# A new instruction order for a fused attention and feed-forward kernel, with one weight load issued later

## The chip, the cores and the metric

The kernel runs on one core of a Trainium2 chip. The metric is the device time of one execution in microseconds (us), as a median of several runs. Profiles are single executions; their span is 1.2 to 1.9 us shorter than the device time of the same run. The engines are TensorE (PE in the profile; PEld is its weight load), VectorE (DVE), ScalarE (ACT), GpSimd (POOL) and SyncE (SP). A "q" behind an engine's name (SPq, ACTq) is its issuing of transfers.

## The reference, cut to what matters

```python
x  = A_x                                    # 2048 x 448, bf16
xn = layernorm(x)
q, k, v = split(xn @ wqkv)                  # 16 heads of 28
pq, pk  = q @ w_phi, k @ w_phi              # per head
phi     = concat(softmax(p), softmax(-p))   # for pq and pk
o       = (phi_q @ (phi_k.T @ v)) / (phi_q @ sum(phi_k))
out     = x + o @ wo + silu(xn @ w1) @ w2   # w1: 448 x 1792
```

x is cut into 16 tiles of 128 rows. "The head" below is the start of the program, until the first three 256-column blocks of `xn @ w1` are done for tiles 0 to 3. It ends with three pairs of 64-row matmuls. "The fold" multiplies w_phi into the transposed q and k weights, about 27 us into the program.

## The kernel before

The program builds a list of operations and orders them itself. Each engine has an in-order list; PE's list follows a written plan from the end of the head. The plan's words: `aF3@4` and `bF3` are the two halves of block 3 of `xn @ w1` in PSUM banks 4 and 5; `aq`, `ak`, `av` are projections; `f2@0` is a part of the fold; `s` and `U` are parts of the attention; `W` and `R` belong to the output projection.

The first loads, in order of issue:

```python
load_x(0, 1); load_x(1, 2); load_x(2, 4)
load(w1_sb[:, 0:2, 0:512], ...,  "w1_0")    # first piece, first half,  256 KB, SP
load(w1_sb[:, 2:4, 0:512], ...,  "w1_0r")   # first piece, second half, 256 KB, SP
load_w1(512, 1024, "act")                   # second piece: "w1_512", 384 KB, ACT;
                                            # its last rows, 128 KB, SP
load_x(4, 8)                                # "x4": 448 KB, SP
load_w1(1024, FF)                           # 768 KB, SP
load_rows4(wv_sb, A_wqkv, 2*D, 3*D, "wv"); load_x(8, 12); ...
# [cut] four small loads of w_phi, issued by POOL at 3 to 6 us, behind "vaug1"
```

A `chain` fixes the order of the named operations on one engine. `ve0` to `ve3` are the standard deviations of tiles 0 to 3 (called variances below), `ev0` to `ev3` evict the transposed tiles:

```python
chain("warm_act w1_512 ve0 ve1 ev0a ev0 ev1 ve2 ve3 ev2 silu_table".split())
byname["w1_512"].deps.add(byname["warm_act"].id)
# [cut]
for word in "tr0a tr0 tr1 00a 10a 01a 11a 00b 10b 01b 11b tr2 20 21 tr3 02 12 22 03 13 23".split():
```

In this last line `tr1` transposes tile 1; `00a` is block 0, tile 0, with the first half of the first w1 piece, `00b` the same with its second half; `20` is block 2, tile 0, the first word that needs the second piece. The kernel before applies the first half to tiles 0 and 1, then the second half to both. ACT issues the second piece as soon as its warm-up is done.

## Time and profile before

| | before |
|---|---|
| median | 150.09 us (3 runs, 149.77 to 150.26) |
| span of the profiled run | 148.3 us |
| first matmul of block 20 | 8.45 us |
| end of the head (first 64-row matmul) | 11.45 us |
| from there to the start of the last matmul | 134.46 us |

Three more views are useful as a base. The first is the PE timeline of the head in the kernel before (start, busy us, engine, line, operation, output<-inputs, number of instructions):

```profile
8.23 0.39 PE L497 MATMUL psum<-ident,RA 128*128 128x128 bf16 x4
8.45 0.83 PE L482 MATMUL psum<-xnT,phT 128*128 128x128 bf16 x12
9.12 0.39 PE L497 MATMUL psum<-ident,RA 128*128 128x128 bf16 x4
9.34 4.03 PE L482 MATMUL psum<-xnT,phT 128*128 128x128 bf16 x50
```

Nothing waits: block 20 runs at 8.45, right behind the transposes of tile 2. The w1 pieces land in a buffer that the profile calls phT, because it is used again later. The second is the page's list of transfers, with KB each and us from issue to landing; this is the second w1 piece:

```profile
phT<-in_B_w_dram ACTq DMA_DIRECT2D x1, 384.0 KB, 4.6
```

The third is the table of stretches of the kernel before. After the stretch come its length, the busy time of PE, PEld, DVE, ACT and POOL, each with its instruction count, the granted TensorE clock, the DMA share and the GB/s:

```profile
4.00:6.00 2.00, 2.00 (x21) 1.77 (x18) 1.89 (x8) 0.88 (x4) 1.95 (x6) 1.00 1.00 335
6.00:8.00 2.00, 1.80 (x23) 1.41 (x22) 1.83 (x8) 1.28 (x4) 0.19 (x1) 1.00 1.08 342
8.00:11.00 3.00, 3.00 (x57) 3.00 (x55) 1.67 (x5) 2.08 (x3) 0.75 (x2) 1.00 1.05 361
11.00:16.00 5.00, 4.93 (x52) 2.29 (x51) 4.41 (x16) 3.77 (x4) 3.18 (x9) 1.00 1.35 256
```

PE is busy in full from 8 us on, and its clock is 1.00 in every stretch. (For the first stretches this column misleads: the trace has no clock event there, and until 6.6 us the matmuls of the head still start about 107 ns apart, later 56 ns.)

### The profile page before, as it was taken

What the parts mean: (1) busy time and instruction counts of PE and PEld (TensorE: products, weight loads), DVE (VectorE), ACT (ScalarE), POOL (GpSimd) and SP (SyncE); (2) the same over time, 40 slices, a digit from 0 to 9 for tenths busy, and PEclk for the clock granted to TensorE, in tenths of its full rate; (3) what the DMA queues carried; (4) which work ended last, traced back from release to release, by engine and by line L of the source; (5) the groups of instructions that cost most, each with busy time, mean ns of one, the idle gap of its engine ahead of it and who ended that gap; (6) DMA issues with size and microseconds to landing.
All of it is one profiled execution on the core that took longest, in us unless ns stands there. A gap on an engine that the chain in (4) does not pass through costs nothing.

```text
span 148.3 us, 3741 instructions
## 1 busy us (share of the span) xinstructions
PE 143.9 (97%) x1572; PEld 80.2 (54%) x1572; DVE 91.3 (62%) x197; ACT 71.8 (48%) x92; POOL 74.1 (50%) x92
## 2 busy tenths in 40 slices
PE   7999999999999999999999999999899999999994
PEld 7894444554544557646444445555455555545573
DVE  2968997380799399407992006995789544225083
ACT  4657656569994699995755599100040000000000
POOL 8628566501099999996999600996001800000000
DMA  4999954899930000000387490086899884305024
GB/s 104 337 359 239 301 106 78 165 117 250 348 96 0 0 0 4 4 0 4 63 153 142 81 136 0 0 164 88 155 210 183 111 156 95 70 4 186 0 68 154
DMA packets 44496, 17.53 MB, mean 118 GB/s; under 512 B 37040, under 2 KB 44096, under 8 KB 44480
## 3 DMA queue, kind: packets, MB, share of 16 engines
q1 hardware_dynamic: 41648, 15.10, 50.0%
q10 hardware_dynamic: 2704, 2.17, 4.8%
q8 instruction: 12, 0.20, 0.5%
q0 software_dynamic: 128, 0.03, 0.1%
q14 instruction: 4, 0.03, 0.1%
HBM read 6.57 MB, written 1.84 MB: 57 GB/s over the span
## 4 chain that ended last, share of the span: by engine, by line
PE 68%; DVE 11%; DMA 8%; SPq 6%; ACT 3%; issue 2%; POOL 1%; ACTq 0%
PE psum L482 68%; SPq L583 5%; DVE Rec L778 4%; DMA phT<-in_B_w_dram 3%; DMA vaug<-vaug 3%; DVE st L643 2%; DMA wT<-in_A_wqkv_dram 2%; DVE RA L658 1%; SPq L516 1%; ACT hT L502 1%; DVE Rec L779 1%; ACT L502 1%; ACT Ek_sb L502 1%; DVE mv L644 1%; DVE x_sb L896 1%
## 5 line engine op out<-in xcount | busy, mean ns | idle before, releaser
L482 PE MATMUL psum<-xnT,phT 64*128 64x512 bf16 (+1 forms) x428 | 45.5, 351 | 0.3 <-DMA phT<-in_B_w_dram 0.2
L482 PE MATMUL psum<-w_sb,hT 128*128 128x448 bf16 (+1 forms) x238 | 45.1, 342 | 0.0
L778 DVE TENSOR_REDUCE Rec<-Ek_sb 128x32 f32<-128x896 bf16 (+1 forms) x20 | 24.4, 1251 | 24.6 <-ACT Ek_sb L502 17.9
L814 POOL TENSOR_TENSOR RA<-Ek_sb,Rec 128x896 bf16<-128x896 bf16 x16 | 27.0, 1722 | 22.0 <-issue 12.0
L502 ACT ACTIVATE hT<-psum 128x1024 bf16<-128x1024 f32 x28 | 27.3, 1023 | 10.9 <-PE psum L482 10.9
L482 PEld LDWEIGHTS psum<-xnT,phT 64*128 64x128 bf16 (+1 forms) x428 | 21.5, 95 | 20.2 <-PE psum L482 0.6
L482 PEld LDWEIGHTS psum<-w_sb,hT 128*128 128x128 bf16 x238 | 22.2, 98 | 18.7 <-issue 1.5
L502 ACT ACTIVATE Ek_sb<-psum 128x864 bf16<-128x864 f32 x24 | 20.2, 915 | 19.1 <-PE psum L482 18.8
L482 PE MATMUL psum<-Wqk,xnT 64*128 64x432 bf16 x224 | 23.3, 343 | 0.1
L482 PEld LDWEIGHTS psum<-Wqk,xnT 64*128 64x128 bf16 x224 | 10.5, 95 | 10.1 <-issue 0.8
L788 POOL TENSOR_TENSOR Ek_sb<-Ek_sb,Rec 128x896 bf16<-128x896 bf16 x8 | 13.3, 1699 | 5.0 <-DVE Rec L779 5.0
L788 POOL TENSOR_TENSOR phT<-phT,Rec 128x896 bf16<-128x896 bf16 x8 | 13.4, 1702 | 0.2 <-DVE Rec L779 0.2
L482 PE MATMUL psum<-wv,xnT 64*128 64x448 bf16 x112 | 12.6, 349 | 0.1
L643 DVE BATCH_NORM_STATS2 st<-x_sb 128x6 f32<-128x448 bf16 x16 | 9.6, 603 | 2.9 <-DMA x_sb<-in_A_x_dram 2.9
L896 DVE TENSOR_TENSOR x_sb<-psum,x_sb 128x448 bf16<-128x448 f32 (+1 forms) x13 | 7.1, 582 | 6.6 <-PE psum L482 6.6
L482 PE MATMUL psum<-wo_sb,vaug 128*128 128x448 bf16 (+1 forms) x51 | 10.5, 341 | 0.5 <-DMA vaug<-vaug 0.5
L874 DVE TENSOR_SCALAR den<-psum 128x16 f32<-128x16 f32 x16 | 2.4, 157 | 13.2 <-PE psum L482 13.2
L881 DVE TENSOR_TENSOR vaug<-psum,rden 128x448 bf16<-128x448 f32 x16 | 9.8, 623 | 0.4
L658 DVE TENSOR_SCALAR RA<-x_sb,mv,rstd 128x384 bf16<-128x384 bf16 (+4 forms) x29 | 8.9, 346 | 1.3 <-POOL rstd L654 1.1
L779 DVE RECIPROCAL Rec<-Rec 128x32 f32<-128x32 f32 (+1 forms) x24 | 8.7, 393 | 0.2
L482 PEld LDWEIGHTS psum<-wv,xnT 64*128 64x128 bf16 x112 | 5.4, 94 | 5.5 <-PE psum L482 0.5
L502 ACT ACTIVATE vaug<-psum 128x896 bf16<-128x896 f32 x8 | 7.4, 923 | 1.7 <-PE psum L482 1.7
(59 smaller groups left out, 113.0 us busy)
## 6 DMA issues: line engine op xcount, KB each, us to landing
out_dram<-x_sb ACTq DMA_DIRECT2D x15, 112.0 KB, 1.7
w_sb<-in_B_w_dram SPq DMA_DIRECT2D x1, 1568.0 KB, 9.4
x_sb<-in_A_x_dram SPq DMA_DIRECT2D x3, 448.0 KB, 5.9
wo_sb<-in_A_wo_dram SPq DMA_DIRECT2D x2, 336.0 KB, 7.6
phT<-in_B_w_dram SPq DMA_DIRECT2D x1, 576.0 KB, 7.0
phT<-in_B_w_dram SPq DMA_DIRECT2D x2, 256.0 KB, 4.4
phT<-in_B_w_dram ACTq DMA_DIRECT2D x1, 384.0 KB, 4.6
wv<-in_A_wqkv_dram SPq DMA_DIRECT2D x1, 336.0 KB, 7.2
```

The lines of the kernel that those rows point to most:

```text
L482: r = e.matmul(dst, lhsT, rhs, start=st, stop=sp, skip_group_check=True)
L502: P.op("act", d_act(n), lambda e: e.activation(dst, src, func, scale=scale), reads=[src], writes=[dst], table=table, name=name, **keys)
L583: o = P.dma(lambda e: e.dma_start_transpose(out=dst, in_=src), xfer, lat=650.0, reads=[src] if kw.pop("sbuf", True) else [], writes=[dst], ...
L643: P.op("dve", 590, lambda e: e.bn_stats(st6[:, t, :], xs), reads=[xs], writes=[st6[:, t, :]], name=f"bnst{t}", okeys_w=["ln"])
L658: P.op("dve", dur, lambda e: e.tensor_scalar(dst, x_sb[:, t, c0:c1], mv[:, t, 0:1], rstd[:, t:t + 1], ALU.subtract, ALU.mult), reads=[xs, ...
L778: P.op("dve", 50 + 967 * n, lambda e: e.tensor_reduce(R2, E4, AXL.X, ALU.add), reads=[E4], writes=[R2], name="Ssum")
L779: P.op("dve", 135 + 210 * n, lambda e: e.reciprocal(R2, R2), reads=[R2], writes=[R2], name="Rrec")
L788: P.op("pool", 1700, lambda e: e.tensor_tensor(E3, E3, Rk[:, :, None].broadcast_to([128, 32, DH]), ALU.mult), reads=[E3, Rk], writes=[E3], ...
L814: P.op("pool", 1700, lambda e: e.tensor_tensor(dst, Eq, Rq.rearrange("p (c j) -> p c j", c=CC)[:, :, :, None].broadcast_to([128, CC, 4, DH ...
L874: P.op("dve", 190, lambda e: e.tensor_scalar(den[:, uq, :], U3[:, :, DH], EPS_DEN, None, ALU.add), reads=[U3[:, :, DH]], writes=[den[:, uq ...
L881: P.op("dve", 620, lambda e: e.tensor_tensor(o3, U3[:, :, 0:DH], rden[:, uq, :, None].broadcast_to([128, H, DH]), ALU.mult), reads=[U3[:, ...
L896: P.op("dve", d_dve(cs.stop - cs.start), lambda e: e.tensor_tensor(res[:, cs], ob, addend[:, cs], ALU.add), reads=[ob, addend[:, cs]], wri ...
```

## The change

The intent is to let attention tiles be transposed longer before they are needed (a new plan and larger expected latencies for these transposes), to use each half of the first w1 piece as soon as it is there, and to make room for that piece's second half by sending the second piece later: behind the first variance, `ve0`, instead of behind the warm-up.

```diff
-PLAN = """aF3@4 bF3 aF4@0 aF6@2 av2@6 ...
+PLAN = """aF3@4 bF3 aF5@0 aF4@2 av0@6 ...          [the whole plan is new]
         load_x(4, 8)
         # [cut] two lines of the program's scheduler, for a third line of transfers
+        early = {o.name: o for o in P.ops}          # what the scheduler expects; it changes no transfer
+        early["w1_512"].crowd = 2
+        early["w1_512"].lat = 1300.0
+        early["x4"].xfer += early["w1_512"].xfer
-            o.lat += 700.0 if name in ("xnT_dma5", "xnT_dma7") else 0.0
+            o.lat += {"xnT_dma5": 700.0, "xnT_dma7": 700.0, "oT_dma": 500.0, "phqT": 500.0}.get(name, 0.0)
-        chain("warm_act w1_512 ve0 ve1 ev0a ev0 ev1 ve2 ve3 ev2 silu_table".split())
-        byname = {o.name: o for o in P.ops}
-        byname["w1_512"].deps.add(byname["warm_act"].id)
-        byname["w1_512"].odeps -= byname["w1_512"].deps
+        chain("warm_act ve0 w1_512 ve1 ev0a ev0 ve2 ev1 ve3 ev2 silu_table".split())
-... "tr0a tr0 tr1 00a 10a 01a 11a 00b 10b 01b 11b tr2 20 21 tr3 02 12 22 03 13 23"
+... "tr0a tr0 tr1 00a 10a 00b 10b 01a 11a tr2 01b 11b 20 21 tr3 02 12 22 03 13 23"
```

More of the change, by code (lines that the diff above doesn't have):

```diff
@@ L241, in schedule @@
         act_table = [None]
-        dma_free = [0.0, 0.0]
+        dma_free = [0.0, 0.0, 0.0]
         order = {e: [] for e in ENGINES}
@@ L305, in schedule @@
                 line = o.crowd
-                if line:
+                if line == 1:
                     issue_end = max(issue_end, dma_free[1] + 300.0)
@@ L333 @@
           ("pool", "pe"): 100.0}
-PLAN = """aF3@4 bF3 aF4@0 aF6@2 av2@6 bF4 bF6 aF5@4 av0@0 bv0 bF5 aF12@2 bv2 aF11@0 aF13@4 bF12 bF11 bF13 aF10@6 aF8@0 f0@2 f3@4
-bF8 bF10 f2@2 aF9@0 f1@4 aF7@6 bF9 bF7 ak2@4 bk2 av12@6 av10@0 ak14@2 bv12 bk14 bv10 ak4@4 av14@6 bk4 ak0@2 bv14 av6@0
-bk0 bv6 Y2@6:5 Y2:6 Y2:3 ak6@2 ak8@0 bk6 av8@4 av4@6 bv8 bk8 bv4 ak10@4 ak12@2 bk10 aq4@0 bk12 K0-2 bq4 aq6@4 K2-6 bq6
-aq8@2 s4 aq0@0 bq8 K6-8 bq0 aF17@4 K8-10 bF17 aF14@2 aF19@0 bF14 bF19 aF16@4 aF23@2 K10-16 bF16 aF27@0 M bF23 bF27
-aF24@5 aF20@2 bF24 aF26@0 bF20 aF15@4 bF26 s6 bF15 aF21@6 aF22@2 bF21 aF18@4 s8 bF22 s0 aF25@0 aq2@6 bF18 bF25 bq2
-aq12@2 aq10@4 bq12 bq10 F9@1:2 F9:4 F9:8 U7 F7@6:10 s2 F7:4 Y1@5:2 Y0@0:6 U4@2 Y0:8 s10 U0@4 Y1:9 U9 Y1:3 F4@0:1 F4:13
-U2 W4 U6@3 U3@5 W7 W9 s12 W0@2 R4,7 aq14@3 R0,9 bq14 Y3@5:2 Y3:3 U5@2 U1 F5@6:5 F5:9 U8@2 F6@0:11 F6:3 Y3:5 U13@2 U11
-F11@4:14 Y3:2 U10@3 s14 W2@2 W5 W6 U12 F14@3:6 F10@1:7 U14 Y3:2 F10:7 F14:6 W10 F13@7:10 F14:2 W11 W14 R6,14 R5,10 R2,11
-F13:4 F8@5:8 F8:4 F8:2 W3@6 W8 W13 F12@1:2 F12:1 F12:11 U15@0 W12 W1@4 R1,8,13 R12,3 F15@23:6 F15:8 E15"""
+PLAN = """aF3@4 bF3 aF5@0 aF4@2 av0@6 bF5 bF4 bv0 aF6@0 av2@4 bF6 bv2 aF13@6 aF11@2 bF13 aF12@4 bF11 aF10@6 bF12 bF10 aF8@0 f2@2
+f0@4 bF8 f3@6 aF7@2 aF9@0 f1@4 bF9 bF7 ak2@4 bk2 av12@6 av10@2 ak14@0 bv12 bk14 bv10 ak4@4 av14@6 bk4 ak0@0 bv14 ak6@2
+bk0 Y2@5:11 Y2:3 bk6 av6@6 ak8@0 bv6 bk8 av8@4 av4@2 ak10@6 bv4 bk10 bv8 ak12@2 aq4@0 bk12 K0-6 bq4 s4 aq8@2 aq6@4 bq8
+K6-8 aq0@0 bq6 bq0 aF14@2 K8-10 bF14 aF17@4 K10-12 aF19@0 bF17 bF19 aF23@2 K12-16 aF20@0 aF18@4 bF20 s6 s8 bF18 bF23
+aF15@0 aF27@4 M bF15 aF25@2 bF27 aF22@0 bF25 s0 aF21@4 aF16@6 bF21 bF22 bF16 aF24@4 aq2@2 aF26@0 bF24 bF26 aq10@6 bq2 s2
+bq10 U9@5 F4@4:14 F5@3:8 F5:6 U0@2 U7 aq14@0 aq12@5 bq14 bq12 s10 Y3@2:8 U5 F7@1:6 F7:6 F0@5:3 F0:2 F0:9 s12 Y3:6 F7:2
+U6@0 U4 W7 W0 F6@6:4 F6:3 W5 F9@0:4 F9:10 W9 F6:7 W6 U10 W4 R5,7 s14 R0,6 R9,4 F13@2:5 F12@1:7 F12:6 Y1@0:3 U15@4 U12@5
+Y1:11 U14 U13@6 F13:9 U8@0 F12:1 F10@3:5 U2@4 F8@6:9 F10:9 F8:2 U3@4 F11@0:3 W13 U1 F8:3 W8 F11:2 F11:9 U11 F14@5:14
+W1@4 W12 W14 R14,12 R1,8,13 W10 W3@7 W11 W2@1 F15@64:2 R10,11 R3,2 F15:6 F15:5 F15:1 E15"""
 def bass_parallel_sum__linear_kernel_hedgehog__dense_activation_silu__prompt_kernel(
@@ L947, in bass_parallel_sum__linear_kernel_hedgehog__dense_activation_silu__prompt_kernel @@
         seq = []
-        for word in "tr0a tr0 tr1 00a 10a 01a 11a 00b 10b 01b 11b tr2 20 21 tr3 02 12 22 03 13 23".split():
+        for word in "tr0a tr0 tr1 00a 10a 00b 10b 01a 11a tr2 01b 11b 20 21 tr3 02 12 22 03 13 23".split():
             if word[0] == "t":
```

## The prediction

> **What bounds the kernel now.** I read the page's busy shares first, then the chain that ended last, then what the TensorE waited for, then the TensorE and SyncE timelines around those waits.
>
> ```profile
> PE 143.9 (97%) x1572; PEld 80.2 (54%) x1572; DVE 91.3 (62%) x197; ACT 71.8 (48%) x92; POOL 74.1 (50%) x92
> PE   7999999999999999999999999999899999999994
> PE 68%; DVE 11%; DMA 8%; SPq 6%; ACT 3%; issue 2%; POOL 1%; ACTq 0%
> ```
>
> TensorE is busy for 97% of 148.3 us, and only its first and last slice are low. No other engine is over 62%. So the change can win only what TensorE loses: real gaps, plus small losses inside "busy". The chain leaves TensorE in the second slice group and again near 85 to 104 us (DVE, DMA), but that counts only where TensorE then really stood still:
>
> ```profile
> PE psum L545 <- POOL epst L509: 1.1, 1, 1.1
> PE psum L482 <- DMA vaug<-vaug: 0.5, 1, 0.5
> PE psum L482 <- DMA wT<-in_A_wqkv_dram: 0.3, 1, 0.3
> PE psum L482 <- DMA phT<-in_B_w_dram: 0.2, 1, 0.2
> ```
>
> That is all: 1.0 us apart from the start-up. The three places on TensorE's timeline, and the SyncE queue that feeds the largest:
>
> ```profile
> 6.11 1.50 PE L482 MATMUL psum<-xnT,phT 128*128 128x128 bf16 x16
> 7.77 0.62 PE L482 MATMUL psum<-xnT,phT 128*128 128x128 bf16 x8 [0.16 <-DMA phT<-in_B_w_dram]
> ...
> 27.61 0.39 PE L482 MATMUL psum<-BD,Y_sb 64*128 64x56 bf16 x16 [0.34 <-DMA wT<-in_A_wqkv_dram]
> ...
> 104.18 0.74 PE L482 MATMUL psum<-wo_sb,vaug 128*128 128x448 bf16 x3 [0.46 <-DMA vaug<-vaug]
> ```
>
> ```profile
> 95.93 1.92 SPq L583 DMA_TRANSPOSE phT<-RA  x1
> 98.45 5.66 SPq L583 DMA_TRANSPOSE vaug<-vaug  x4
> ```
>
> The reader is to see at 7.77 the second half of the first w1 piece coming late, at 27.61 the nine transposed wqkv tiles, at 104.18 the output projection waiting for a transposed attention tile whose issue stood in a full transpose queue (1.26 to 1.9 us of SyncE per issue).
>
> Matmul ends are modelled and overlap the next start by 163 ns, so a "gap" understates the loss. Start to start is better. A warm 128-column matmul starts 55.6 ns after the last, a 448-column one 189 ns, a pair of 64-row 512-column ones 216 ns. Against these paces TensorE loses, in the kernel before: 1.4 us in the head (5.09 to 11.29); 0.50 before the fold at 27.61; 0.24 at 29.98 (a bank whose SiLU eviction is not done); 0.17 at 33.5 (the last fold subtraction on VectorE); 0.61 at 103.6; three times 0.23 where the second half of a block follows its own first half with rows and banks swapped; and five pairs of changes between 128-row and 64-row matmuls at 0.096 + 0.106.
>
> **What the Trainium skill says.** "TensorE: Matmul & The Clock Gate", section "Wait — 56ns, not 53.3ns?": N / 2.4 GHz + 2.5 ns start to start when warm, N / 1.2 GHz cold. The trace agrees: 55.6, 189 and 216 ns; the first ten head matmuls run at 90 to 107 ns, until about 6.6 us. "TensorEngine Tiling (Array Packing)", "Key Properties": a change of tiling mode drains the array. The trace shows that as 0.2 us a pair. "DMA: Bandwidth & Descriptors", "Queues, rings and completion order": SP and ACT own one row each on the same 16 DMA engines, and an engine takes rows in turn, a whole packet at a time. This decides the second w1 piece. The trace fits, without proving it: that piece (issued by ACT at 2.33) moved its 384 KB at 4.6 to 6.0 us, between the two halves of the first piece (issued by SP at 2.19 and 2.67; they moved at 3.7 to 4.9 and 5.8 to 6.8). Strict order of issue would look the same.
>
> **The change, part by part.** It adds and removes no matmul: 1572 in both orders, same shapes, so the paced sum (136.2 us from the first transpose) stays. DVE, ACT, POOL and SP get the same instructions in another order. What can move is the loss.
>
> 1. *The head.* Before, the second half landed at 7.72 us because 384 KB of the second piece went in front of it. At the 340 or so KB/us of that stretch, sending them later frees 1.1 us: it lands near 6.6. The new order is tile 0 with both halves, then tile 1. TensorE does the four-plus-four first-half matmuls of tile 0 from 6.11 to 6.8, then the four of the second half to 7.0, then waits for tile 1 of the transposed input. ACT now puts the third variance (0.29) ahead of that eviction, so it ends near 7.25 instead of 6.93. From 7.3: eight matmuls (0.45), the transposes of tile 2 (0.22), four (0.22): the second piece's block starts at 8.2 instead of 8.44. **Gain 0.2.** It needs the second piece by 8.2. ACT now issues it at about 4.15; by turns it moves at 6.0 to 7.1, in front of the 448 KB x load, and lands by 8.0. In strict order of issue it moves behind that load, at 7.1 to 8.2, and lands near 9.0: then the head **loses** 0.6.
>
> 2. *The fold.* The first fold moves one block half later (8 matmuls, 0.86 us). The transposed wqkv must land by 27.6 as before; the fold would now be due at 27.61 - 0.50 + 0.86 - 0.23 (item 3) - 0.2 = 27.5. **The 0.50 goes, or nearly.** But two fold pairs and the block reuse now stand closer. From the end of a block whose bank is wanted again there is 0.234 + 0.648 = 0.88 us of work; before it was 1.10 and lost 0.24, so 1.34 is needed and 0.46 is lost: **0.22 worse.** The wait for the last fold subtraction stays near 0.17: six subtractions of one fold pair take 2.3 us on DVE (28.32 to 30.60) in either order.
>
> 3. *Swaps and modes.* Two swaps in place of three: **-0.23.** Six mode pairs in place of five, since the late q blocks no longer share a stretch with the 64-row remainders: **+0.20.**
>
> 4. *Transposes.* The first output projection used a tile normalised 7.2 us of paced work earlier; it stalled 0.61. In the new order its nearest tile lies 11 us back, and no projection has under 6 us. The last pair of q blocks is projected some 12 us earlier, so their transposes leave before the rush. **-0.61.** I take off 0.15 for new small waits: the tile normalised behind four DVE sums at about 97 us is wanted again at about 107, and its transpose stands behind a 1.9 us one.
>
> 5. *The tail.* The last tile is still split over two banks; 2.1 us from the last matmul's end to the end of the span stays.
>
> Sum: -0.2 - 0.5 + 0.22 - 0.23 + 0.20 - 0.61 + 0.15 = about -1.0 with the second piece in time, about -0.2 with it late.
>
> **The rivals.** *A late second w1 piece* takes the place of the late first one. For it: its issue-to-landing was 4.6 us before, and 4.15 + 4.6 = 8.75 is after 8.2. Against: half of that was queueing behind loads that are by then done, and the change's own bookkeeping puts it on a line of its own and delays the x load instead, which nobody would write for a piece that goes last. I give it one in four; the time is then near 149.9. *A new stall of the transposes*: the SyncE queue still issues the same 16 output and 11 attention transposes, and the DVE sums still precede some normalisations. A wait like the old one would give back 0.3 to 0.6: 149.6. *The gain is hidden anyway*: if the fold still waits for the transposed wqkv (its queue is serial on SyncE from 17.42, driven by DVE), a head gain of 0.2 buys nothing there; already counted as "nearly". *Another engine as bound*: DVE at 62% and POOL at 50% have room; I see none. A gain over 2% would need 3 us; all real gaps together are 1.0 us and all listed losses about 4.6, most of which stay.
>
> **Range and chances.** 0.75 x -1.0 + 0.25 x -0.2 is -0.8, from the median of 150.09: 149.2. Run-to-run spread is 0.5. Low 148.5: all gaps gone with nothing new. High 150.1: late piece and one new stall. Over 2% either way would need a term that I can't find in the trace: 0.02 faster, 0.95 the same, 0.03 slower.
>
> **What would show it.** TensorE's waits without the vaug line and with the wT line gone or under 0.1; tile 0's second-half matmuls before 7.1 us and a continuous head from about 7.3; the second piece's DMA moving before the x load and no wait at 8.2; about 0.4 of idle time within 2 us behind the first fold; an output projection with no idle before it. The prediction is wrong if the head shows a wait for w1 over 0.3 us, if a wait for phT or vaug transposes over 0.5 us appears after 85 us, or if the paced sum changes.

## The result, and the profile after

The changed kernel takes 154.58 us (median of 4 runs, 153.59 to 155.99), the kernel before 149.94 us in the same rounds (4 runs, 149.77 to 150.26). The ratio is 1.029, with a 95% interval of 1.023 to 1.034: slower. A ratio here is the mean time of one kernel's fast runs over that of the other's of the same rounds, so it is not quite the ratio of the medians that are quoted.

From the page of the changed kernel: the busy shares, PE in 40 slices, PE's clock in the same slices, the DMA engines in the same slices, and the engines' shares of the chain that ended last.

```profile
PE 144.7 (95%) x1572; PEld 81.3 (54%) x1572; DVE 91.0 (60%) x196; ACT 71.6 (47%) x92; POOL 74.0 (49%) x92
PE   7729999999999999999999999999999999999994
...
PEclk9996899999999999999999999999999999999999
DMA  4999765499940000000068792139937945452144
...
PE 89%; DMA 6%; DVE 2%; ACT 1%; issue 0%; ACTq 0%
```

The hole is in the third slice (7.6 to 11.4 us), where PE is busy for a fifth of the time. The next two slices have a lower clock: 0.6 and 0.8. After that, PE is full to the end; the slice with an 8 near 105 us in the kernel before is gone. PE's waits, with total, number and longest:

```profile
PE psum L482 <- DMA phT<-in_B_w_dram: 3.5, 2, 2.7
...
PE psum L482 <- DVE Wqk L640: 0.3, 1, 0.3
```

The waits for the attention transposes (vaug) and for the transposed qkv weights (wT) are gone, as the change wanted. In their place w1 costs 3.5 us in two waits. The PE timeline of the changed kernel shows where:

```profile
5.99 0.62 PE L482 MATMUL psum<-xnT,phT 128*128 128x128 bf16 x8
7.41 0.83 PE L482 MATMUL psum<-xnT,phT 128*128 128x128 bf16 x12 [0.80 <-DMA phT<-in_B_w_dram]
8.07 0.39 PE L497 MATMUL psum<-ident,RA 128*128 128x128 bf16 x4
8.30 0.39 PE L482 MATMUL psum<-xnT,phT 128*128 128x128 bf16 x4
11.39 0.84 PE L482 MATMUL psum<-xnT,phT 128*128 128x128 bf16 x12 [2.71 <-DMA phT<-in_B_w_dram]
```

0.80 us go to the first piece's second half, which landed at 7.27 us (before: 7.72). 2.71 us go to the second piece ahead of block 20. The chain that ended last names that transfer (start, us, what), and the list of transfers gives it 7.5 us where it had 4.6:

```profile
3.88 7.46 DMA phT<-in_B_w_dram
...
phT<-in_B_w_dram ACTq DMA_DIRECT2D x1, 384.0 KB, 7.5
```

The table of stretches of the changed kernel, with the same columns as before:

```profile
4.00:6.00 2.00, 2.00 (x22) 1.72 (x19) 1.89 (x8) 0.90 (x4) 1.96 (x6) 1.00 0.97 268
6.00:8.00 2.00, 1.20 (x22) 1.06 (x20) 1.86 (x8) 1.23 (x4) 0.19 (x1) 1.00 0.96 315
8.00:11.00 3.00, 0.69 (x13) 0.51 (x10) 0.13 (x1) 2.08 (x3) 0.14 (x1) 1.00 1.06 369
11.00:16.00 5.00, 4.61 (x54) 4.41 (x56) 3.43 (x11) 0.00 (x0) 2.48 (x8) 0.67 1.25 292
```

The last line is the second loss. From 11 to 16 us PE is "busy" for 4.61 of 5 us, so the busy time hides it; the clock of 0.67 does not. Start to start, 29 matmuls of the head take 107 ns each in place of 56.

The balance, from first-matmul times of both traces:

| | before | after | difference |
|---|---|---|---|
| block 20 starts | 8.45 | 11.39 | +2.94 |
| from there to the end of the head | 3.00 | 4.55 | +1.55 |
| end of the head to the last matmul's start | 134.46 | 133.53 | -0.93 |

Their sum, 3.56, is the 3.5 us by which the profiled span grew (148.3 to 151.8). The head loses almost five times what is gained behind it. The 0.93 is not all the plan's own: 0.50 of it is the wait ahead of the fold, which is gone here because the head is late (`e1_order` shows the plan alone).

### The profile page after: what moved, and what is told of

It reads as the page before. It is cut to its first block, busy times and chain, and to the rows that moved or that the text cites. A ratio compares the mean times of both kernels' runs of the same rounds, so it can differ in the third digit from the quotient of the medians.

```text
span 151.8 us, 3736 instructions
## 1 busy us (share of the span) xinstructions
PE 144.7 (95%) x1572; PEld 81.3 (54%) x1572; DVE 91.0 (60%) x196; ACT 71.6 (47%) x92; POOL 74.0 (49%) x92
## 3 DMA queue, kind: packets, MB, share of 16 engines
HBM read 6.57 MB, written 1.84 MB: 55 GB/s over the span
## 4 chain that ended last, share of the span: by engine, by line
PE 89%; DMA 6%; DVE 2%; ACT 1%; issue 0%; ACTq 0%
PE psum L482 88%; DMA phT<-in_B_w_dram 5%; DMA x_sb<-in_A_x_dram 1%; ACT hT L502 1%; DVE Wqk L640 1%; DVE x_sb L900 1%; DVE st L647 0%; PE psum L497 0%; DVE mv L648 0%; ACT last_hi L502 0%; ACT last_lo L502 0%; ACTq L1110 0%; ACT ve L651 0%
## 5 line engine op out<-in xcount | busy, mean ns | idle before, releaser
L482 PE MATMUL psum<-xnT,phT 64*128 64x512 bf16 (+1 forms) x428 | 47.2, 356 | 3.9 <-DMA phT<-in_B_w_dram 3.5
L502 ACT ACTIVATE hT<-psum 128x1024 bf16<-128x1024 f32 x28 | 27.3, 1024 | 17.5 <-PE psum L482 17.5
L482 PEld LDWEIGHTS psum<-xnT,phT 64*128 64x128 bf16 (+1 forms) x428 | 22.5, 98 | 23.8 <-DMA phT<-in_B_w_dram 2.9
L782 DVE TENSOR_REDUCE Rec<-phT 128x64 f32<-128x1792 bf16 x4 | 8.0, 2007 | 0.6 <-ACT phT L502 0.6
```

The lines of the kernel that those rows point to most:

```text
L482: r = e.matmul(dst, lhsT, rhs, start=st, stop=sp, skip_group_check=True)
L502: P.op("act", d_act(n), lambda e: e.activation(dst, src, func, scale=scale), reads=[src], writes=[dst], table=table, name=name, **keys)
L782: P.op("dve", 50 + 967 * n, lambda e: e.tensor_reduce(R2, E4, AXL.X, ALU.add), reads=[E4], writes=[R2], name="Ssum")
```

## The experiments

The first theory after the result was: the late second piece costs the wait and the clock drop behind it, and everything else in the change is a gain of about 0.9 us. The rivals were that the new head order or the new plan has its own part in the loss. The second question was why the piece takes 7.5 us. Sixteen kernels ran, in four groups, each on one chip; the median of the kernel before was 149.78, 149.49, 149.91 and 149.39 us in the four groups. All kernels gave correct results. A run is called slow when it is over 1.5% above the fastest of its kernel; what the slow runs here have in common is said under "Wait or clock".

### The parts one by one

`e1_order`: the kernel before with the new plan and the new expected latencies alone.

```diff
-PLAN = [before]   ... 700.0 if name in ("xnT_dma5", "xnT_dma7")
+PLAN = [after]    ... {"xnT_dma5": 700.0, ..., "oT_dma": 500.0, "phqT": 500.0}
```

> The new order of the blocks alone; head and w1 pieces as in the kernel before. Theory A (the order wins, the late second w1 piece loses): the wait for the transposed attention tile at 104 us and the one before the fold go, about 1.0 us faster than before, 148.9 us, head unchanged (first 64-row matmul at 11.4 us). Rival B (the order itself costs time behind the head): same or slower than before, 150 us or more.

149.56 us (6 runs, 149.45 to 150.34), ratio 1.001 (0.998 to 1.004). In the profile the head is that of before (end 11.57 us), and 133.88 us follow it, 0.58 fewer. PE's waits in this run:

```profile
PE psum L482 <- DMA wT<-in_A_wqkv_dram: 0.4, 1, 0.4
PE psum L482 <- DVE Wqk L636: 0.2, 1, 0.2
```

The vaug wait is gone. The wait ahead of the fold is not, although the fold stands one block half later: it starts at 28.38 us, because the transposed weights land later too. So the plan is worth about 0.6 us in a profile, which the runs cannot tell from nothing.

`e2_late`: the kernel before with the second piece alone moved behind `ve0`.

```diff
-chain("warm_act w1_512 ve0 ve1 ev0a ev0 ev1 ...")   [and its dependence on warm_act]
+chain("warm_act ve0 w1_512 ve1 ev0a ev0 ev1 ...")   [and the bookkeeping lines]
```

> The kernel before with only the second w1 piece sent behind the first variance; old order, old sequence in the head. Theory A: the piece lands at 11 to 11.5 us instead of 7.0, TensorE waits about 2.9 us for it and then runs some 30 matmuls at half clock (1.6 us): about 4.5 us slower than before, 154.5 us. Rival C (the piece is late only together with the new sequence in the head): within 1 us of before.

153.63 us (4 runs, 152.33 to 155.84), ratio 1.024 (1.019 to 1.028). Its profile fell in the slow state, so only its order of events is used: the piece landed at 13.1 us, and PE waited for it. So this one line makes the slowdown, or nearly all of it: the whole change has 1.029, and the two intervals overlap.

`e3_early`: the changed kernel with the second piece sent early again.

```diff
-chain("warm_act ve0 w1_512 ve1 ev0a ev0 ve2 ev1 ve3 ev2 silu_table")
+chain("warm_act w1_512 ve0 ve1 ev0a ev0 ve2 ev1 ve3 ev2 silu_table")   [and as before]
```

> The changed kernel with the second w1 piece sent at once again. Theory A: no wait for the second piece, no drop of the clock; but tile 0 now waits for the second half of the first piece until 7.7 us with nothing else to do, so the head ends 0.4 us later than before and the order gives back 1.0: 149.4 us. Rival B: over 150.5 us.

149.83 us (6 runs, 149.62 to 150.04), ratio 1.001 (0.999 to 1.004), clock 1.000 in every run. The new head order alone is a small loss: tile 0's second-half matmuls are now first in line for a piece half that still lands late, and wait 1.15 us in one go until 7.96; the head ends at 12.07. That is 0.6 us later than before, where 0.4 was expected, and behind the head 0.65 us come back (133.81), where 1.0 was expected.

### Wait or clock

`e4_fill`: the changed kernel with 48 matmuls into an unused bank ahead of block 20. They take 2.84 us, most of the wait, so PE stays at work while the piece is as late as ever.

```diff
+for n in range(48):   # ones x ones, 128 columns, each 56 ns
+    P.op("pe", 56.0, lambda e: e.matmul(banks[5][:, 0:128], ones_bf[:], ones_bf[:], start=True, stop=True), ...)
+at = seq.index("F20_0"); seq[at:at] = [f"fill{n}" for n in range(48)]
```

> The changed kernel with 48 idle-filling matmuls (about 2.7 us of work that nothing uses) where TensorE waits for the second piece. Theory A: the second piece lands when it did (11.3 us), but the clock stays at full, so the 31 matmuls at 107 ns go back to 56 ns: 1.6 us faster than the changed kernel, about 153.0 us. Rival D (the clock drop has another cause than the idle wait, such as its place in the window): still about 154.5 us, or slower if the fillers delay the block.

153.13 us (4 runs, 152.41 to 153.63), ratio 1.023 (1.020 to 1.026). Clock and PE timeline of this kernel:

```profile
PEclk9999999999999999999999999999999999999999
```

```profile
8.60 2.84 PE L936 MATMUL psum<-ones_bf 128*128 128x128 bf16 x48
12.23 0.84 PE L482 MATMUL psum<-xnT,phT 128*128 128x128 bf16 x12 [0.79 <-DMA phT<-in_B_w_dram]
```

From block 20 to the end of the head it takes 3.01 us, as before (3.00) and not 4.55. The granted clock is 0.998 to 1.000 in its four runs, where the changed kernel has 0.978 to 0.989. So the clock drop is a consequence of PE's standing still, and costs 1.55 us. The piece came 0.84 us later in this run than in the changed kernel's, and the kernel was no slower for it.

The clock records of the traces add a detail that the averages hide. Each drop that they record in a head lasts 3.41 us (12.65 to 16.06 us in the changed kernel, 12.27 to 15.69 in `e5_hold`, 7.77 to 11.19 in `e6_sp`), or twice that (`e2_late`, `e7_x0`). In the changed kernel it begins 1.26 us after block 20 did, not in the wait. In the 3.41 us before these drops PE was busy for 1.26, 1.07 and 1.83 us. Where it was busy for 2.62 of 3.41 us (`e4_fill`, from 11.26 us on) no drop followed; but none followed 1.68 us either (`e15_x4smallwp`, from 6.54 us on), so this share alone does not decide it. Half the clock for 3.41 us takes 1.1% off the mean clock of a run, so in the run lists 1.000 means no drop, 0.989 one and 0.978 two. Every run that counts as slow here has at least one drop more than the fastest run of its kernel.

### What else shares the engines

`e5_hold`: the changed kernel with all SP loads behind x4 held until the second piece has landed.

```diff
+for n in ("w1_1024", "w1_1024r", "wv", "wvr", "x8"):
+    byname[n].deps.add(byname["w1_512"].id)
```

> The changed kernel, with SyncE holding every load behind the second x load until the second w1 piece has landed (its total time is not the question: SyncE's queue shifts by some us). Theory T1 (the late piece is slow because it shares the DMA engines by turns with the loads that SyncE issued before and after it): with only the 448 KB x load beside it, the 384 KB land by 9.0 to 9.5 us instead of 11.3, and TensorE waits under 1.0 us for them. Rival T2 (its own queue is slow when it is issued late, whatever runs beside it): still 11 us or later.

One look: 154.22 us, state unknown. The piece landed at 11.22. The loads behind x4 are not what makes it late. In the table of stretches the engines even fall idle while it is still under way:

```profile
8.00:11.00 3.00, 0.94 (x17) 0.76 (x14) 0.11 (x1) 2.08 (x3) 0.00 (x0) 1.00 0.48 174
```

A transfer is spread over 16 engines, and its 16 completion marks in the trace came between 8.84 and 11.22: the last ones are late, not all.

`e6_sp` puts the second piece on SP's queue behind the first piece; `e7_x0` leaves it on ACT's queue, but issues it when x0 has landed.

```diff
-load_w1(512, 1024, "act")                      # e6_sp; "w1_512" leaves ACT's chain
+load_w1(512, 1024)
+byname["w1_512"].deps.add(byname["x0"].id)     # e7_x0; "w1_512" stands ahead of ve0 again
# [cut] in both, the bookkeeping lines are out
```

> The changed kernel with the second piece issued by SyncE right behind the first, so that all loads of the head are in one queue. T1: in one queue nothing overtakes, so it lands before the x load, at 8.5 to 9.2 us, TensorE waits under 0.7 us, no half clock: 149.5 us or less. If one queue alone leaves the DMA engines partly idle between 4.6 and 6.6 us (as in all runs with the late piece), the second half of the first piece still lands at 7.3 us.

> The changed kernel with the second piece issued by ACT behind the landing of the first x tile (2.9 us), that is just behind the second half of the first piece instead of just in front of it. T1: it meets only that half and the small rest of its own rows, lands at 7.5 to 8.5 us, no wait over 0.3 us: 149.0 us. T2 (late means slow): lands after 9 us, waits 1 us or more.

`e6_sp`: 149.63 us (4 runs, 148.98 to 150.62), ratio 1.000 (0.997 to 1.004). `e7_x0`: 152.09 us (4 runs, 150.67 to 153.41), ratio 1.015 (1.010 to 1.019). The issue times are close: 2.90 us for `e7_x0`, and the third of four issues that start at 2.20 and take 1.99 us for `e6_sp`, so about 3.2. Yet the piece landed at 10.4 us in `e7_x0` and at about 8.8, 5.6 us behind its issue, in `e6_sp`. T1 was met in full by neither: PE still waited 1.31 us in the profile of `e6_sp`, and that run had a drop of the clock (0.989; its other three runs have 1.000). The Trainium skill, "DMA: Bandwidth & Descriptors", section "Issuing engines are not separate DMA queues", says that transfers of all issuing engines interleave on the same 16 engines, and that issuing from several of them only saves the sequencer's time. Interleaving fits these two runs, but there is more than the sequencer's time in it: in SP's own queue, where it stands ahead of x4, the second piece came sooner although it was issued later, and so did the first piece's second half (7.67 us against 8.82). That the place ahead of x4 is the reason is argued here; the last group of experiments bears on it.

`e8_swap`: the second half of the first piece goes on ACT's queue at once, and the second piece takes its place on SP's.

```diff
-load(w1_sb[:, 2:4, 0:512], ..., "w1_0r")
+load(w1_sb[:, 2:4, 0:512], ..., "w1_0r", "act")
-load_w1(512, 1024, "act")
+load_w1(512, 1024)                             [chain: w1_0r in w1_512's early place]
```

> The changed kernel with the two transfers swapped: ACT issues the second half of the first piece at once, SyncE the second piece behind the first half. If what is issued at 2.3 us by the second queue fills the engines (as the second piece did before: 384 KB by 7.0 us), the 256 KB of the half land by 6.5 to 6.9 us, tile 0 goes through without a wait at 6.9, the second piece lands by 8.3: head 0.2 to 0.4 us shorter than before and the order's 0.6 on top: 148.9 to 149.2 us. If not, the half lands at 7.3 or later and the time is that of the run with the second piece at once, 149.8 us.

149.18 us (6 runs, 148.79 to 149.81), ratio 0.999 (0.996 to 1.002). The half landed at 6.81, near what the change had wanted, block 20 started at 8.45 as before, and the clock stayed at 1.000. The head, expected 0.2 to 0.4 us shorter, ends at 11.45 as before. Behind it the plan's gain is down to 0.2 us (134.24), with 0.88 us lost ahead of the fold.

### The small loads of GpSimd, and the spread of one kernel

In the late kernels, packets of POOL's four small loads took up to 1.3 us, where most packets take 0.05 to 0.2. The theory was that they block the rings of some engines. Three kernels move these loads behind the head, with the same edit:

```diff
-chain(["vaug1", "wphi", "wphi1", "wphi2", "wphi3"])
+chain(["rstd7", "wphi", "wphi1", "wphi2", "wphi3"])
```

`e9_wplate` is the changed kernel with it, `e10_swapwp` is `e8_swap` with it, `e11_beforewp` the kernel before with it.

> The changed kernel with one edit: the four small loads that GpSimd issues at 3 to 6 us (the packed w projection rows) are chained behind the last rstd instead of vaug1, so that they start after the head. Theory T3 (their slow packets hold up some DMA engines' rings while the late piece is waiting): the first piece's second half lands at 6.7 or earlier, the late w1 piece lands by 8.5 us, PE waits under 0.5 us for it, no clock drop, median 148.5 to 149.5. Rival T2 (the piece is late by its own place: issued on the second queue after SP's loads are in the rings, it takes about 7 us whatever else is under way): lands at 10.5 us or later, PE waits over 2 us, about 30 half-rate matmuls, median 153.5 to 155.

> The changed kernel with the two w1 loads swapped between queues (as e8_swap) and GpSimd's small loads behind the last rstd. The candidate for best. T3: a little better than e8_swap, 148.5 to 149.1, ratio to the kernel before 0.993 to 0.997. T2 and the others: as e8_swap, ratio 0.997 to 1.001. Block 20 starts at 8.4 or earlier, the head's last matmul at 11.4.

> The kernel before with GpSimd's small loads behind the last rstd: what they cost where the w1 piece goes early. T3: the w1 rings end a little sooner, head 0 to 0.3 us shorter, 149.2 to 149.8. T2: no change, ratio 0.998 to 1.002.

`e9_wplate`: 154.39 us (4 runs, 151.76 to 155.45; two of them count as slow and no ratio was given; the run of 151.76 had no drop of the clock). The piece landed at 11.64, so the theory falls as it was put. `e10_swapwp`: 149.63 us (6 runs, 148.87 to 150.03), ratio 0.997 (0.994 to 0.9995). `e11_beforewp`: 149.69 us (4 runs, 149.6 to 149.78), ratio 0.998 (0.995 to 1.000). Neither is outside 2%; `e10_swapwp` is the only one whose interval lies below 1, by very little. Its profile has the head that the prediction wanted: the first piece's second half landed at 6.45 us, block 20 started at 8.22 and the head ended at 11.22, 0.23 us earlier than in the kernel before. In `e11_beforewp` the head ended at 11.74, so POOL's loads alone do not shorten it.

`e0_before` is an unchanged copy of the kernel before, for a second profile.

> An unchanged copy of the kernel before, for a second profile: how far the landing of the transposed qkv weights, and so the wait ahead of the fold (503 ns in the first profile, 520 in e1_order, 457 in e3_early, 881 in e8_swap, 0 where the head is long), moves between runs of one kernel. If it is set by the head's length and not by chance: fold wait 450 to 560 ns, head's last 64-row matmul at 11.4 to 11.6. If it is chance: anywhere from 0.2 to 0.9. Time 149 to 150.3.

150.13 us, span 148.8. The head ends at 11.50, as in the first profile, but the wait ahead of the fold is not the same. PE's waits in this run:

```profile
PE psum L482 <- DMA wT<-in_A_wqkv_dram: 0.9, 1, 0.9
PE psum L482 <- DMA phT<-in_B_w_dram: 0.4, 1, 0.4
PE psum L482 <- DMA vaug<-vaug: 0.2, 1, 0.2
```

Start to start it is 1.11 us, against 0.50 in the first profile. So the size of this wait is partly chance, and the fold times of two single profiles cannot be compared to better than some 0.6 us. The wait for a transposed attention tile varies too: 0.2 us here and 0.5 in the first profile of the same kernel. Over all profiles whose head ends by 12.1 us, and in which no load is held, 134.36 to 134.99 us follow the head with the old plan (three profiles) and 133.81 to 134.30 with the new one (four). The new plan is ahead in every pair of these, but by anything from 0.1 to 1.2 us.

### Everything out of the way

The last four kernels take away, in steps, what could share the engines with the late piece. `e12_alone` is the changed kernel with x4 and all later SP loads held until the piece has landed, and POOL's small loads late. `e13_holdx4` is the same, but POOL's loads stay. `e14_x4small` leaves all loads where they are and cuts x4 into four loads of one tile, whose packets have 896 bytes in place of 3,584. `e15_x4smallwp` is that with POOL's loads late. In the expectations, T4 is the theory that an engine takes one packet of each queue in turn, so that a neighbour with larger packets gets more of it; T5 is that POOL's small loads hold back some of the engines besides; T2 is, as above, that the piece is late by its own place.

```diff
+for n in ("x4", "w1_1024", "w1_1024r", "wv", "wvr", "x8"):   # e12, e13
+    byname[n].deps.add(byname["w1_512"].id)
-load_x(4, 8)                                                 # e14, e15
+for t in range(4, 8):
+    load_x(t, t + 1)
-chain(["vaug1", "wphi", ...])                                # e12, e15
+chain(["rstd7", "wphi", ...])
```

> The changed kernel with everything that could share the engines with the late w1 piece held back: x4 and all later SP loads until it has landed, GpSimd's small loads behind the last rstd. T4 and T5: the piece starts near 6.2 us, moves its 384 KB in about 1.1 us and lands by 7.8; block 20 starts at 8.2 to 8.5, no clock drop; the time depends then on the held loads, 149 to 151. T2: lands at 9.5 us or later although nothing else is under way, PE waits over 1.5 us.

> As e12 but with GpSimd's small loads where the changed kernel has them. T4: lands as in e12, by 8 us. T5: some rings stay behind, landing 9 to 10.5. T2: as e12, late.

> The changed kernel with the load x4 cut into four loads of one tile, so that its packets have 896 bytes instead of 3584; bytes and order on the queue unchanged. T4: one packet of the piece now goes against 896 bytes: at 46 + 41 ns a pair, 24 packets of an engine take 2.1 us, it lands at 8.4 to 9.0; PE waits 0.2 to 0.8 us, half-rate matmuls under 10, median 149.5 to 151. T5: 9 to 10.5. T2: unchanged, 11 or later, 153.5 to 155.

> e14 with GpSimd's small loads behind the last rstd as well. T4 and T5: lands at 8.4 to 9.0, median 149.3 to 150.5. T2: 10.5 or later, about 154.

The times: `e12_alone` 153.14 us (4 runs, 152.8 to 153.56), ratio 1.025 (1.021 to 1.029); `e13_holdx4` 153.16 (one look); `e14_x4small` 152.01 (4 runs, 150.84 to 153.59), ratio 1.014 (1.007 to 1.022), its profile in the slow state; `e15_x4smallwp` 151.28 (4 runs, 150.29 to 153.24), ratio 1.010 (1.005 to 1.015). For the landing the piece's own records say more. The table counts the packets of 1,024 bytes in ACT's queue (384 in all) and the 16 completion marks of the piece:

| kernel | what is out of the way | KB moved by 8.0 us | marks, first to last (us) |
|---|---|---|---|
| changed kernel | nothing | 128 | 9.52 to 11.34 |
| `e5_hold` | the loads behind x4 | 143 | 8.84 to 11.22 |
| `e9_wplate` | POOL's small loads | 128 | 8.79 to 11.64 |
| `e14_x4small` | x4 in small packets | 305 | 7.61 to 11.19 |
| `e15_x4smallwp` | that, and POOL's loads | 286 | 7.73 to 9.93 |
| `e13_holdx4` | x4 and the loads behind it | 374 | 7.68 to 8.66 |
| `e12_alone` | all of these | 384 | 7.22 to 8.31 |

The PE timeline of `e12_alone`, in which block 20 is part of the group of 16 at 7.96, and its line in the list of transfers:

```profile
7.03 0.86 PE L482 MATMUL psum<-xnT,phT 128*128 128x128 bf16 x12 [0.43 <-DMA phT<-in_B_w_dram]
7.73 0.39 PE L497 MATMUL psum<-ident,RA 128*128 128x128 bf16 x4
7.96 1.25 PE L482 MATMUL psum<-xnT,phT 128*128 128x128 bf16 x16
```

```profile
phT<-in_B_w_dram ACTq DMA_DIRECT2D x1, 384.0 KB, 4.4
```

The theory that the piece is late by its own place in the program falls: issued at the same 3.88 us it takes 4.4 us with nothing beside it, and the head ends at 11.37 without a clock drop in it. It is the company of x4 that makes it late: with x4 there, uncut, it lands at 11.2 or later (`e5_hold`, `e9_wplate`), with x4 held it lands at 8.66 even with POOL's loads around (`e13_holdx4`). In time `e12_alone` gains nothing, since the held loads are now late for what follows: 137.33 us pass behind the head instead of 133.53. PE waits 1.84 us for a later w1 piece at 15.8 us, and a drop of the clock follows from 15.93 to 19.34.

How x4 does it is shown in part. In the changed kernel, between 7.2 and 7.6 us, the engines ended 31 packets of the piece and 30 of x4: about one for one, 31 KB against 105. With x4 in small packets it was 82 against 35, and the piece had moved 305 KB by 8.0 us in place of 128. So the size of the neighbour's packets has a part in the share. But the rule that I had expected of it, one packet for one packet, gives a landing of 8.4 to 9.0 us, and `e15_x4smallwp` missed that at 9.93: twelve of the 16 marks are there by 8.71, the last four lag. Here is its wait, the longest one seen to leave the clock alone:

```profile
9.98 0.84 PE L482 MATMUL psum<-xnT,phT 128*128 128x128 bf16 x12 [1.66 <-DMA phT<-in_B_w_dram]
```

**Still open:** why the last of the 16 marks come so late (at 11.34 us, 0.8 behind the one before it, in the changed kernel; 1.7 behind it in `e14_x4small`; from 10.45 to 11.22 with half-idle engines in `e5_hold`), and why the engines moved only 229 to 304 GB/s at 4 to 6 us (268 in the changed kernel) in all profiles in which ACT issued nothing at 2.3 us, against 312 to 339 (335 in the kernel before) where it did. No experiment took these apart.

## Why the prediction was wrong

- **The step that failed is the head (part 1).** It had block 20 start at 8.2 us, with the second piece landed by 8.0, and in the worst case by 9.0 with 0.6 us lost. The piece landed at 11.34. The prediction let it move "in front of the 448 KB x load"; it moved beside it, with about a quarter of the bytes in the stretch quoted above, and finished last. Both of its cases, by turns or in strict order, took the engines' full rate for one transfer after the other. It also took the scheduler's bookkeeping as evidence of what the chip does.
- **A term was missing: the clock.** The sum had only waits. PE's stop cost 2.94 us by block 20's start, and 1.55 us more behind it at half the clock (`e4_fill` shows both separately). The Trainium skill's page "TensorE: Matmul & The Clock Gate" was used for the paces only. Its section "HAM oscillation — how this bites in real kernels" says that an idle gap of more than about 3.4 us makes PE cold again. That figure would have given no warning: the rival allowed a wait of some 0.6 us, and even the 2.71 us that came lie under it.
- **The rival was named and mis-sized.** "A late second w1 piece" was given one in four, with a landing at 4.15 + 4.6 = 8.75 us. The issue came at 3.88 and the transfer took 7.46. Half of the 4.6 was thought to be queueing that would be gone; it was replaced by longer queueing.
- **The first piece's second half** was to land near 6.6; it landed at 7.27. The engines carried 268 GB/s at 4 to 6 us and not the 340 of the estimate, and its last two completion marks came 0.5 us behind the others (6.65, then 7.16 and 7.27); which of the two counts for more was not tested. The wait of 0.80 for it was seen by no step. Its size matters little, because block 20 was late anyway.
- **The fold (part 2)** had the right end for a wrong reason. Its wait went from 0.50 to 0, but since the head was 4.5 us longer; in `e1_order`, with a head of normal length, 0.52 stayed. The rival "the fold still waits for the transposed wqkv" was right there. The loss at the block that is wanted again grew from 0.24 to 0.55 us (0.46 predicted), and to 0.458 in `e1_order`.
- **Swaps, modes and transposes (parts 3 and 4)** held. Two clashes in place of three: 0.70 to 0.47 us, the -0.23 of the prediction. The output projection's 0.61 went, in `e1_order` too, and no new wait came; but the 0.61 was the highest of four profiles with the old plan (waits of 0.5, 0.4, 0.2 and 0.2 us). Six mode pairs cost about 0.16 us more than five (0.88, taken net of one misplaced record in the old trace, to 1.04), against 0.20. The sum behind the head is -0.93, where the prediction's own terms give -0.77; 0.50 of each is the fold's wait, which the late head removed.
- **What would show it** was right as a test: a wait for w1 over 0.3 us in the head is there, 3.5 in all.
- **Two slips changed nothing.** By its own terms the forecast is 149.3 us, not 149.2. And not ten but about fourteen of the first head matmuls ran at the slow pace before 6.6 us.

## What to carry to other kernels

Sending a transfer later to make room for another changes its company: look at which other transfers will be under way at the new time, and in what packet size, before taking its old duration or the engines' full rate for it. A wait on TensorE in the microsecond range is not only its own length: look at the clock row of the page and at the stretches behind the wait. And an order that gains some 0.6 us in a profile may still not show in the runs, because another wait (here the one ahead of the fold) varies by as much; so test each part of such a change alone, and profile one kernel twice.

## What the Trainium skill lacked or had wrong

- "DMA: Bandwidth & Descriptors", "Queues, rings and completion order": it says that an engine takes its queue rows in turn, but gives no consequence for shares. Here a transfer with 1,024-byte packets beside one with 3,584-byte packets moved 128 of 384 KB by 8.0 us; beside 896-byte packets 305; alone 384. A figure for the spread of the 16 completion marks of one transfer is not there either; here it reached 2.4 and 3.6 us (8.84 to 11.22, 7.61 to 11.19).
- The same page, "Issuing engines are not separate DMA queues": issuing on several engines is said to save only sequencer time. The second piece on SP's queue, ahead of x4 (issued at about 3.2 us), gave 149.63 us; on ACT's queue, beside it (issued at 2.90), 152.09. So the choice of the queue also sets what a transfer shares the engines with.
- "TensorE: Matmul & The Clock Gate", "HAM oscillation — how this bites in real kernels": it gives about 3.4 us as the idle gap to avoid. Here gaps of 2.71 us (the changed kernel) and 2.33 us (`e5_hold`) were enough to halve the pace of the matmuls behind them, and one of 1.66 us (`e15_x4smallwp`) was not. In the profile of `e6_sp` the twelve matmuls behind a gap of 1.31 us took 1.44 us in place of 0.83, so the length of one gap does not decide it alone. The half pace cost 1.55 us.
